# A fused windowed attention and softplus feed-forward kernel: the opening in another order, with clamps, low parts and divisions on GpSimd and chunk 1 laid out as chunk 0

## Chip, cores and metric

One core of one Trainium2 chip. The metric is the device time of one execution in microseconds (us), lower is better. The engines are PE (TensorE, matrix products), DVE (VectorE), ACT (ScalarE), POOL (GpSimd) and SP, which here only issues transfers. On each engine instructions run in the order in which the program has them; semaphores make them wait for other engines and for transfers.

## Reference

Attention over 8 batches, 8 heads, 576 positions and head dimension 64, in which heads 0 to 3 see a window of 32 positions and heads 4 to 7 every fourth position of a window of 128; its output (4608 tokens of 512 features) goes through a feed-forward layer of 2048 hidden features with softplus. All in float32.

```python
scores = scale * np.matmul(q, k.transpose(0, 1, 3, 2))
mask_plain = (rel >= 0) & (rel < window)
mask_dil = (rel >= 0) & (rel < window * dilation) & (rel % dilation == 0)
scores = np.where(masks[None, :, :, :], scores, -1000000000.0)
attn = np.exp(scores - np.max(scores, axis=-1, keepdims=True))
attn = attn / (np.sum(attn, axis=-1, keepdims=True) + 1e-09)
x = np.matmul(attn, v)                      # to 4608 x 512
h = x @ w_in
g = np.maximum(h, 0.0) + np.log1p(np.exp(-np.abs(h)))
out = g @ w_out
```

## The kernel before

The 4608 tokens are nine chunks of 512. A chunk has four attention groups of two heads (0 and 1 plain, 2 and 3 dilated); group n of the program is group n % 4 of chunk n // 4. A feed-forward slot is one chunk with one of 16 blocks of 128 hidden features (`ff`): in the first 22 slots these are blocks 0 to 4 of chunk 0, blocks 0 to 9 of chunk 1 and blocks 5 to 11 of chunk 0. [...]

The weights come as float64 words. Each of the 32 tiles (block `ff`, `i` = 0 for w_in, 1 for w_out) is decoded in seven steps by `decode_step` (L221): step 0 takes the absolute value on ACT (L229), step 1 clamps it to the exponents of float32 (L231), step 2 shifts (L235), steps 3 and 4 bring in the low bits and the sign (L240, L245), all on DVE; step 5 rounds to the high part on ACT (L252), step 6 subtracts it for the low part on DVE (L255).

The order of everything up to the 22nd slot is written out by hand, as a string of tokens, `OPENING` (L97), which the loop at L891 reads. Each token emits its instructions, and instructions that share an engine keep the order of the tokens. What follows is ordered by a planner, which starts at the 22nd slot and does not look back. The tokens, with n the group, i the slot and m or kt a quarter of a product:

- `q`, `k`, `v`, `m`, `r`: loads of queries, keys, values, masks and of one raw weight tile, issued by SP (only `k0` by ACT). `load_dma` (L195) lets six of the first 90 SP loads be under way: the seventh waits for the first.
- `S` scores with the mask added as a matmul (PE), `M` their maxima (DVE, L478), `N` or `Np` the factor 1/8 on DVE or POOL (L499), `E` eight exponentials with row sums (ACT, L518), `Ep` the sums' 1e-9 on POOL (L529), `Z` the reciprocal (DVE).
- `Pv` divides the 128 by 512 weights on DVE (L540); `T` turns them with four PE transposes, `C` copies them out of PSUM (ACT, L589); `V` is the product with the values (PE, L598), `Xt` a DVE transpose, `Xh` and `Xl` the high part (ACT, L714) and low part (DVE, L718) of the result. Quarters kt = 0 and 1 of a slot need groups 0 and 1 of its chunk, quarters 2 and 3 groups 2 and 3.
- `W` (`shares`, L651): in the geometry of the later chunks ("by head") the division comes after `V`, as eight ACT instructions that read the result from PSUM, each scaled by one column of reciprocals (L658); `Xt` then reads what they wrote. Before the change chunk 1 (groups 4 to 7) has this geometry, set by `BY_HEAD = 1`; chunk 0 divides with `Pv`.
- `H` is a quarter of the first product of a slot (three matmuls of 512 columns into `h_ps`), `A` three ACT passes for the softplus, `G` its last step (DVE, L773), `Gs` and `Gl` its high and low part (ACT L779, DVE L785), `O` a quarter of the second product (`o_ps`).
- `D0_ff_i` to `D5_ff_i` and `Dl` are the decode steps, `F` and `f` products that nobody reads.

POOL does only the small `Np` and `Ep` in the opening; later it subtracts weight blocks (L920). `PLACES` (L46) says in which PSUM banks a group has its scores, its turned weights and its result: `h` the two banks of `h_ps`, `o` those of `o_ps`, `a` the attention's own.

```python
            if self.by_head:
                by_block = self.v.rearrange("p i r d -> p (i r) d")
...
                divided = nc.scalar.activation(
                    out=self.x[:, n], in_=self.values_in[h][:, at_col : at_col + D], func=AF.Copy,
                    scale=self.ri[:, n : n + 1],
                )
```

Of the kernel before, what the change touches and what calls it, by code (L numbers as in the profile page):

```python
# [98 lines left out]
D3_1_0 q3 k3 S3 M3 E0 Pv1 q2 Np3 E3 Ep3 k2 S2 Z0 Pv0 T0 C0 q4 q5 m1 v0 k4 r2 r3 V0 D4_0_0 D5_0_0 M2 Np2 E2
Ep2 D4_1_0 D5_1_0 Z3 Pv3 Xt0 Xh0 D0_0_1 Dl0_0 S4 M4 Dl1_0 D0_2_0 T1 C1 Z2 Pv2 D1_0_1 D2_0_1 Np4 E4 Ep4  # L100
D1_2_0 Xl0 v1 V1 Xt1 Xh1 k5 D2_2_0 D3_2_0 S5 M5 Np5 Xl1 r4 v3 v2 r5 r6 q6 T2 D0_1_1 D3_0_1 D1_1_1 T3 C3 C2
H0_0 D2_1_1 E5 Ep5 F1_0 D4_2_0 D5_2_0 V3 Xt3 Xh3 V2 Xt2 Xl3 D4_0_1 D0_3_0 Xh2 Xl2 D1_3_0 Z4 D0_2_1 D1_2_1 Z5
T5 C5 H1_0 H0_1 T4 C4 D2_3_0 Dl2_0 D3_3_0 D4_3_0 D5_0_1 Dl0_1 H0_2 H0_3 A0 D3_1_1 G0 H1_1 H1_2 H1_3 A1 G1
D2_2_1 D5_3_0 Dl3_0 r7 k6 v4 v5 r8 q7 r9 r10 r11 S6 M6 Np6 V4 W4 D0_4_0 Gs0 Gs1 Xt4 Xh4 D4_1_1 Xl4 Gl0
D1_4_0 Gl1 D2_4_0 D3_2_1 D3_4_0 D4_4_0 D0_4_1 D5_1_1 Dl1_1 E6 Ep6 V5 W5 Xt5 H2_0 H2_1 H2_2 H3_0 H2_3 O0_0
D1_4_1 O0_1 H3_1 H3_2 H3_3 k7 S7 r12 r13 r14 O1_0 O1_1 O0_2 O0_3 M7 Np7 A2 G2 D4_2_1 O1_2 O1_3 D5_4_0 Dl4_0
A3 G3 Xh5 D2_4_1 Xl5 H4_0 H4_1 H4_2 H4_3 D3_4_1 D5_2_1 D0_3_1 Gs2 Gl2 D1_3_1 Dl2_1 O2_0 D2_3_1 D3_3_1 r15 E7
D4_4_1 Z6 D0_5_0 T6 H5_0 H5_1 D1_5_0 D0_6_1 v6 C6 V6 Ep7 Z7 O2_1 D1_6_1 D2_6_1 D4_3_1 A4 W6 Gs3 O2_2 O2_3 k8
v7 r16 r17 G4 D3_6_1 D4_6_1 Gl3 Xt6 T7 D0_5_1 D5_4_1 D1_5_1 D2_5_1 H6_0 H6_1 C7 V7 D5_3_1 Dl3_1 O3_0 O3_1
O3_2 O3_3 Xh6 Xl6 Gs4 W7 Gl4 Dl4_1 O4_0 O4_1 Xt7 Xh7 D2_5_0 D5_6_1 D0_7_0 D0_6_0 Xl7 H5_2 D3_5_0 D1_7_0  # L110
D3_5_1 D1_6_0 D4_5_1 D2_7_0 H5_3 A5 H6_2 H6_3 A6 m2 r18 q8 D4_5_0 D2_6_0 O4_2 r19 r20 K2 S8 G5 O4_3 G6
D3_7_0 D4_7_0 D3_6_0 Dl6_1 H7_0 H7_1 H8_0 H8_1 H7_2 H8_2 H7_3 H8_3 Gs5 K3 Gl5 K0 O5_0 D5_7_0 D5_5_1 Dl5_1
# [1980 lines left out]
```

## Time and profile before

| what | value |
|---|---|
| median of 3 runs | 823.47 us (821.29 to 823.65) |
| the profiled execution's own time | 822.52 us |
| its span, first to last instruction | 820.7 us |
| PE busy | 800.1 us, 97% |
| DVE busy | 648.1 us, 79% |
| ACT busy | 614.8 us, 75% |
| POOL busy | 63.9 us, 8% |
| moved by transfers | 198.45 MB, mean 242 GB/s |

All times inside the profile count from the span's start; 1.8 us of the execution's time lie outside it. "Busy" is a share of time, not of speed: a PE that runs at half clock counts as busy. The opening ends at about 166 us, when POOL begins to subtract weight blocks.

### The profile page before, as it was taken

What the parts mean: (1) busy time and instruction counts of PE and PEld (TensorE: products, weight loads), DVE (VectorE), ACT (ScalarE), POOL (GpSimd) and SP (SyncE); (2) the same over time, 40 slices, a digit from 0 to 9 for tenths busy, and PEclk for the clock granted to TensorE, in tenths of its full rate; (3) what the DMA queues carried; (4) which work ended last, traced back from release to release, by engine and by line L of the source; (5) the groups of instructions that cost most, each with busy time, mean ns of one, the idle gap of its engine ahead of it and who ended that gap; (6) DMA issues with size and microseconds to landing.
All of it is one profiled execution on the core that took longest, in us unless ns stands there. A gap on an engine that the chain in (4) does not pass through costs nothing.

```text
span 820.7 us, 19960 instructions
## 1 busy us (share of the span) xinstructions
PE 800.1 (97%) x7849; PEld 650.6 (79%) x7849; DVE 648.1 (79%) x945; ACT 614.8 (75%) x1468; POOL 63.9 (8%) x88
## 2 busy tenths in 40 slices
PE   5899999999999999999999999999999999999998
PEld 3677888888888877778888888888888888888886
DVE  5888988857587789778789998777798967667964
ACT  6999889867777777699899837887897345776732
POOL 1000000031335433000000000000000000000000
PEclk8799999999999999999999999999999999999999
DMA  8994835375999989657787968998776576666652
GB/s 299 314 313 138 283 101 177 121 241 186 339 297 342 318 317 341 234 173 224 255 274 246 310 226 272 288 308 289 242 244 210 189 242 205 204 193 212 223 198 85
DMA packets 105807, 198.45 MB, mean 242 GB/s; under 512 B 9585, under 2 KB 52593, under 8 KB 105713
## 3 DMA queue, kind: packets, MB, share of 16 engines
q1 hardware_dynamic: 105568, 196.88, 73.2%
q8 instruction: 62, 1.02, 0.5%
q14 instruction: 33, 0.26, 0.1%
q10 hardware_dynamic: 144, 0.29, 0.1%
HBM read 148.90 MB, written 48.23 MB: 240 GB/s over the span
## 4 chain that ended last, share of the span: by engine, by line
PE 94%; ACT 2%; DVE 2%; DMA 0%; issue 0%; POOL 0%; SPq 0%; DVEq 0%; ACTq 0%; POOLq 0%
PE o_ps L261 44%; PE h_ps L261 16%; PE h_y L261 14%; PE h_x L261 14%; PE sv_ps L261 5%; ACT s L518 1%; PE s_ps L261 1%; PE a_ps L261 1%; DMA k<-kpl 0%; PE t_ps L551 0%; DVE a L381 0%; ACT pt L658 0%; DVE s L381 0%; ACT pt L589 0%; DVE nm L478 0%
## 5 line engine op out<-in xcount | busy, mean ns | idle before, releaser
L261 PE MATMUL o_ps<-g,t 128*128 128x512 f32 x867 | 208.9, 389 | 0.0
L261 PEld LDWEIGHTS o_ps<-g,t 128*128 128x128 f32 x867 | 161.9, 188 | 34.3 <-DVE g L1502 0.2
L261 PE MATMUL o_ps<-g,parts 128*128 128x512 f32 x576 | 144.1, 393 | 0.2 <-DVE g L785 0.2
L261 PE MATMUL h_ps<-xh,parts 128*128 128x512 f32 x384 | 130.9, 397 | 1.1 <-DVE e L773 1.1
L261 PEld LDWEIGHTS o_ps<-g,parts 128*128 128x128 f32 x576 | 106.9, 188 | 24.0 <-DVE g L785 0.7
L1498 ACT CAST g<-stored 128x1024 fp32r<-128x1024 f32 x72 | 75.7, 1052 | 60.2 <-PE o_ps L261 56.6
L1502 DVE TENSOR_TENSOR g<-stored,g 128x1024 fp32r<-128x1024 f32 x72 | 87.8, 1221 | 26.1 <-ACT g L1498 25.9
L261 PEld LDWEIGHTS h_ps<-xh,parts 128*128 128x128 f32 x384 | 73.0, 190 | 17.4 <-DVE e L773 1.6
L518 ACT ACTIVATE s<-s,nm 128x64 f32<-128x64 f32 x224 | 75.7, 358 | 2.2 <-DVE nm L507 1.3
L261 PE MATMUL h_ps<-xl,parts 128*128 128x512 f32 x192 | 75.7, 394 | 0.0
L261 PE MATMUL h_y<-s,t 128*128 128x512 f32 x276 | 70.6, 391 | 0.0
L261 PE MATMUL h_x<-s,t 128*128 128x512 f32 x276 | 70.5, 391 | 0.0
L920 POOL TENSOR_TENSOR a<-a 128x256 f32<-128x256 f32 x64 | 56.8, 895 | 100.5 <-DVE a L915 81.5
L261 PEld LDWEIGHTS h_x<-s,t 128*128 128x128 f32 x276 | 51.6, 188 | 11.0
L261 PEld LDWEIGHTS h_y<-s,t 128*128 128x128 f32 x276 | 51.5, 188 | 10.9
L1478 DVE SCALAR_TENSOR_TENSOR stored<-stored,e 128x1024 f32<-128x1024 f32 x48 | 58.3, 1217 | 2.4 <-ACT e L1474 2.4
L1493 DVE TENSOR_TENSOR stored<-stored 128x1024 f32<-128x1024 f32 x48 | 58.1, 1215 | 0.2
L658 ACT ACTIVATE pt<-sv_ps,ri 128x64 f32<-128x64 f32 x224 | 49.0, 331 | 9.6 <-DVE s L484 6.7
L1468 ACT ACTIVATE e<-stored 128x1024 f32<-128x1024 f32 x48 | 50.6, 1056 | 3.0 <-DVE stored L1457 2.3
L1474 ACT ACTIVATE e<-e 128x1024 f32<-128x1024 f32 x48 | 50.7, 1061 | 1.0
L1471 ACT ACTIVATE e<-e 128x1024 f32<-128x1024 f32 x48 | 50.8, 1058 | 0.7
L773 DVE SCALAR_TENSOR_TENSOR e<-h_ps,e 128x512 f32<-128x512 f32 x48 | 32.9, 686 | 23.0 <-ACT e L1173 17.3
(112 smaller groups left out, 1260.0 us busy)
## 6 DMA issues: line engine op xcount, KB each, us to landing
t<-w_o SPq DMA_DIRECT2D x84, 512.0 KB, 4.3
raw<-w SPq DMA_DIRECT2D x64, 256.0 KB, 5.3
v<-vp SPq DMA_DIRECT2D x28, 512.0 KB, 5.5
t<-w SPq DMA_DIRECT2D x20, 512.0 KB, 4.1
t<-w_two SPq DMA_DIRECT2D x20, 512.0 KB, 4.4
k<-kl SPq DMA_DIRECT2D x31, 320.0 KB, 4.8
q<-qp SPq DMA_DIRECT2D x35, 256.0 KB, 4.2
w_o<-stage SPq DMA_DIRECT2D x32, 256.0 KB, 4.6
```

Source lines behind the costliest of these rows:

```text
L261: return tc.keep_in_program_order(nc.tensor.matmul(**kw))
L518: pin(nc.scalar.activation(out=self.blocks[:, t], in_=src, func=AF.Exp, bias=self.nm[:, t : t + 1], scale=1.0 / 8.0 if self.masked else 1. ...
L658: divided = nc.scalar.activation(out=self.x[:, n], in_=self.values_in[h][:, at_col : at_col + D], func=AF.Copy, scale=self.ri[:, n : n + 1],)
L773: pin(nc.vector.scalar_tensor_tensor(out=e, in0=tiles.pop(i), scalar=0.0, in1=e, op0=ALU.max, op1=ALU.add))
L920: pin(nc.gpsimd.tensor_tensor(out=out, in0=in0, in1=in1, op=ALU.subtract))
L1468: pin(nc.scalar.activation(out=es[key], in_=raw_g(*key), func=AF.Abs))
L1471: pin(nc.scalar.activation(out=es[key], in_=es[key], func=AF.Exp, scale=-1.0))
L1474: pin(nc.scalar.activation(out=es[key], in_=es[key], func=AF.Ln, bias=1.0))
L1478: pin(nc.vector.scalar_tensor_tensor(out=h, in0=h, scalar=0.0, in1=es.pop(key), op0=ALU.max, op1=ALU.add))
L1493: pin(nc.vector.tensor_tensor(out=raw_g(c, *PLACE[name]), in0=raw_g(c, *PLACE[a]), in1=raw_g(c, *PLACE[b]), op=op))
L1498: pin(nc.scalar.copy(out=set_of(k)[0], in_=raw_g(c, *PLACE[name])))
L1502: pin(nc.vector.tensor_tensor(out=low, in0=raw_g(c, *PLACE[name]), in1=high.bitcast(F32), op=ALU.subtract))
```

## The change

The string `OPENING` is another one, and so is `PLACES`. New tokens `Ba` and `Bl` are the clamp (step 1) and the low part (step 6) of a weight tile on POOL, the old token `P` divides on POOL. Counted in the new order, 19 clamps, 23 low parts and 5 divisions (groups 1, 2, 3, 4 and 7) are on POOL; groups 0, 5 and 6 divide on DVE. `BY_HEAD` is gone: chunk 1 is masked, divided, turned and read from PSUM as chunk 0 is, so its 32 ACT divisions go, and its `Xt` reads PSUM. The layout of its keys, queries and values on the host changes with it, the small tile `spread` is no longer loaded with the identity (128 by 640 instead of 128 by 768 elements of bfloat16), and its mask is added by a matmul with the identity over 128 rows instead of 32. The same loads, products and decode steps are done; one full product that nobody reads and the 21 small ones stand now at the program's start. The instructions behind the opening are the same ones in the same order on every engine.

```diff
-PLACES = "hoa oaa oao aoa haa ooa oaa aaa".split()
+PLACES = "aoa oao aoa hoo oaa hoa aaa oaa".split()
 FIRST = 2
-BY_HEAD = 1
...
 OPENING = """
-q1 k1 m0 S1 M1 q0 k0 S0 M0 N0 r0 r1 D0_0_0 D1_0_0 D2_0_0 D3_0_0 f21 Np1 E1 Ep1 Z1 D0_1_0 D1_1_0 D2_1_0
...
+q0 F1_1 m0 f21 k0 S0 M0 N0 k1 E0 k3 q3 S3 M3 Np3 E3 Ep3 m1 q1 q2 k2 S1 Z0 Pv0 T0 r0 r1 M1 Np1 k4 q4 Z3 P3 r2
...
-    def decode_step(ff, i, step):
+    def decode_step(ff, i, step, engine=None):
...
         elif step == 1:
-            pin(nc.vector.tensor_scalar(
+            pin((engine or nc.vector).tensor_scalar(
                 out=a, in0=a, scalar1=W_MIN, scalar2=W_MAX, op0=ALU.max, op1=ALU.min
...
             parts = words[key][3]
-            pin(nc.vector.tensor_tensor(
+            pin((engine or nc.vector).tensor_tensor(
                 out=parts[:, 1], in0=a, in1=parts[:, 0].bitcast(F32), op=ALU.subtract
...
-            self.own, self.masked, self.by_head = c == 0, c < 2, c >= BY_HEAD
+            self.own, self.masked = c == 0, c < 2
...
             first = True
-            if self.by_head:
+            if self.c >= FIRST:
                 by_block = self.v.rearrange("p i r d -> p (i r) d")
...
         "O": o_part,
+        "Ba": lambda ff, i: decode_step(ff, i, 1, nc.gpsimd),
+        "Bl": lambda ff, i: decode_step(ff, i, 6, nc.gpsimd),
         "Dl": lambda ff, i: decode_step(ff, i, 6),
```

What moves, at three places. First PE, from the last transposes ahead of the feed-forward products on (`t_ps` the transposes, `a_ps` the value products, `h_ps` the `H` quarters, `unread` a product that nobody reads). Before:

```order
L551 MATMUL t_ps<-ident,s 128x128 x8
L261 MATMUL h_ps<-xh,parts 128x512
L261 MATMUL h_ps<-xl,parts 128x512
L261 MATMUL h_ps<-xh,parts 128x512
L261 LDWEIGHTS consts
L261 MATMUL unread<-consts 128x512
L261 MATMUL a_ps<-v,pt 32x2x32 x64
L551 MATMUL t_ps<-ident,s 128x128 x4
```

and in the change:

```order
L542 MATMUL t_ps<-ident,s 128x128 x4
L259 MATMUL s_ps<-k,q 32x64 x32
L259 LDWEIGHTS consts
L259 MATMUL s_ps<-mask,consts 128x256
L542 MATMUL t_ps<-ident,s 128x128 x12
L259 MATMUL a_ps<-v,pt 32x2x32 x96
L259 MATMUL h_ps<-xh,parts 128x512
L259 MATMUL h_ps<-xl,parts 128x512
L259 MATMUL h_ps<-xh,parts 128x512 x2
```

The first `H` quarter no longer stands ahead of `V3` and `V2` but behind all three of `V1`, `V3`, `V2` (32 rows each), and the full unread product between them is gone from here.

Second POOL, from its first small instructions on. Before it has these alone:

```order
L499 TENSOR_SCALAR nm<-nm 128x8
L529 TENSOR_SCALAR sm<-sm 128x8
L499 TENSOR_SCALAR nm<-nm 128x8
L529 TENSOR_SCALAR sm<-sm 128x8 x5
L920 TENSOR_TENSOR a<-a 128x256 x64
```

and in the change, from its first division on:

```order
L531 TENSOR_TENSOR s<-s,ri 128x512
L490 TENSOR_SCALAR nm<-nm 128x8
L520 TENSOR_SCALAR sm<-sm 128x8
L229 TENSOR_SCALAR a<-a 128x512
L490 TENSOR_SCALAR nm<-nm 128x8
L531 TENSOR_TENSOR s<-s,ri 128x512 x2
L229 TENSOR_SCALAR a<-a 128x512
L531 TENSOR_TENSOR s<-s,ri 128x512
L253 TENSOR_TENSOR parts<-a,parts 128x512
```

The divisions (L531) stand in one queue with clamps (L229), low parts (L253) and the small factors (L490, L520) that ACT and DVE wait for.

Third ACT, from the first softplus (`e`) of the feed-forward on. Before:

```order
L766 ACTIVATE e<-h_ps 128x512
L767 ACTIVATE e<-e 128x512
L768 ACTIVATE e<-e 128x512
L252 CAST parts<-a 128x512
L658 ACTIVATE pt<-a_ps,ri 128x64 x8
L229 ACTIVATE a<-raw 128x512
L779 CAST g<-e 128x512 x2
L714 CAST xh<-s 128x8x64
```

and in the change:

```order
L753 ACTIVATE e<-h_ps 128x512
L754 ACTIVATE e<-e 128x512
L755 ACTIVATE e<-e 128x512
L580 COPY pt<-t_ps 128x512
L250 CAST parts<-a 128x512
L701 CAST xh<-s 128x8x64
L766 CAST g<-e 128x512
```

The eight divisions that read the result of `V` (L658) are gone; the copy of the turned weights (L580) takes a place of its own.

## Rows read from the trace of the kernel before

**Rows 1.** The page: span, busy time, and 40 slices of PE and its clock
```profile
span 820.7 us, 19960 instructions
PE 800.1 (97%) x7849; PEld 650.6 (79%) x7849; DVE 648.1 (79%) x945; ACT 614.8 (75%) x1468; POOL 63.9 (8%) x88
...
PE   5899999999999999999999999999999999999998
...
PEclk8799999999999999999999999999999999999999
```

**Rows 2.** Windows: stretch, length; busy PE, PEld, DVE, ACT, POOL; clock, DMA share, GB/s
```profile
14.00:27.70 13.70, 11.18 (x342) 8.28 (x342) 12.54 (x30) 12.46 (x61) 2.46 (x7) 0.50 0.93 305
27.70:39.60 11.90, 11.11 (x229) 8.03 (x228) 10.03 (x22) 10.61 (x31) 0.53 (x2) 0.91 0.88 297
39.60:48.85 9.25, 6.95 (x145) 5.48 (x144) 7.87 (x17) 9.22 (x37) 0.44 (x2) 0.82 0.98 324
48.85:166.00 117.15, 117.15 (x1115) 94.12 (x1114) 103.43 (x195) 102.49 (x267) 2.28 (x6) 1.00 0.56 179
166.00:300.00 134.00, 134.00 (x1497) 109.93 (x1496) 96.09 (x160) 100.09 (x290) 48.44 (x56) 1.00 0.87 290
```

**Rows 3.** PE's timeline to 50 us: start, length, engine, line, what [idle before <-releaser]
```profile
5.22 1.17 PE L261 MATMUL s_ps<-k,q 64*32 64x64 f32 x64 [5.22 <-DMA k<-kpl]
...
27.77 0.78 PE L261 MATMUL h_ps<-xh,parts 128*128 128x512 f32 x1
...
31.67 0.82 PE L261 MATMUL a_ps<-v,pt 64*32 64x64 f32 x60 [0.62 <-ACT s L518]
...
38.51 0.86 PE L261 MATMUL s_ps<-keys 64*32 64x64 f32 x64
...
39.61 0.86 PE L261 MATMUL a_ps<-v,pt 64*32 64x64 f32 x64
42.75 1.35 PE L261 MATMUL a_ps<-v,pt 64*32 64x64 f32 x64 [2.28 <-ACT pt L658]
44.03 0.79 PE L261 MATMUL h_ps<-xh,parts 128*128 128x512 f32 x1
...
48.85 1.52 PE L261 MATMUL o_ps<-g,parts 128*128 128x512 f32 x6
50.21 0.39 PE L261 MATMUL h_ps<-xh,parts 128*128 128x512 f32 x1
```

**Rows 4.** ACT's timeline, the first exponentials of a group to the next work; one W
```profile
9.11 0.30 ACT L518 ACTIVATE s<-s_ps,nm 128x64 f32<-128x64 f32 x1
...
11.43 0.72 ACT L229 ACTIVATE a<-raw 128x512 f32<-128x512 f32 x1
...
40.96 1.74 ACT L658 ACTIVATE pt<-a_ps,ri 128x64 f32<-128x64 f32 x8
```

**Rows 5.** Groups by line to 300 us: form, count | busy us, mean ns | idle before
```profile
L920 POOL TENSOR_TENSOR a<-a 128x256 f32<-128x256 f32 x56 | 48.7, 875 | 93.8 <-DVE a L915 75.1 <-DVE parts L942 13.2 <-DVE sm L529 3.2
L255 DVE TENSOR_TENSOR parts<-a,parts 128x512 fp32r<-128x512 f32 x32 | 21.5, 683 | 0.4 <-ACT parts L252 0.3
L915 DVE TENSOR_TENSOR a<-parts 128x512 f32<-128x512 f32 x28 | 20.6, 759 | 0.0
L231 DVE TENSOR_SCALAR a<-a 128x512 f32<-128x512 f32 x32 | 13.2, 412 | 1.1 <-ACT a L229 1.0
L942 DVE TENSOR_TENSOR stage<-a,stage 128x512 fp32r<-128x512 f32 x16 | 11.6, 748 | 0.0
L303 POOL MEMSET consts<- 128x512 bf16 x1 | 0.5, 525 | 0.3 <-POOLq L2075 0.3
```

**Rows 6.** POOL and DVE timelines: POOL with DVE quiet, POOL and DVE at once
```profile
199.06 0.75 POOL L920 TENSOR_TENSOR a<-a 128x256 f32<-128x256 f32 x1 [22.62 <-DVE a L915]
306.60 8.48 POOL L920 TENSOR_TENSOR a<-a 128x256 f32<-128x256 f32 x8 [6.38 <-DVE a L915]
310.25 1.23 DVE L785 TENSOR_TENSOR g<-e,g 128x512 fp32r<-128x512 f32 x1
```

More of the change, by code (lines that the diff above doesn't have):

```diff
@@ L97 @@
 OPENING = """
-q1 k1 m0 S1 M1 q0 k0 S0 M0 N0 r0 r1 D0_0_0 D1_0_0 D2_0_0 D3_0_0 f21 Np1 E1 Ep1 Z1 D0_1_0 D1_1_0 D2_1_0
[L99 to L112, printed above, removed]
@@ new lines @@
+r3 S2 M2 Np2 D0_0_0 D1_0_0 D2_0_0 E1 Ep1 D3_0_0 D0_1_0 Ba1_0 Z1 E2 Ep2 D4_0_0 D2_1_0 D0_0_1 Ba0_1 C0 D0_2_0 S4
+M4 D3_1_0 Np4 E4 Z2 P2 P1 Ba2_0 D2_0_1 D3_0_1 D4_0_1 v0 V0 Xt0 T3 C3 D4_1_0 Xh0 Ep4 Z4 Xl0 P4 q5 k5 S5 D5_0_0
+M5 Bl0_0 Np5 D2_2_0 T1 C1 D5_1_0 T2 C2 T4 C4 v1 r4 V1 D0_1_1 Xt1 D3_2_0 Bl1_0 Ba1_1 Xh1 Xl1 E5 Ep5 v3 V3 Xt3
+Xh3 v2 V2 Xt2 Xh2 D2_1_1 H1_0 H0_0 H0_1 q7 r5 r6 k7 H1_1 Xl3 Xl2 H1_2 H1_3 D4_2_0 H0_2 S7 D0_3_0 Z5 Pv5 D3_1_1
+D0_2_1 Ba3_0 D2_3_0 D3_3_0 D4_3_0 D5_0_1 Bl0_1 D5_2_0 Bl2_0 T5 A1 G1 D4_1_1 C5 H0_3 q6 v5 V5 Xt5 Ba2_1 A0 G0
@@ new lines @@
+M7 D5_3_0 Xh5 Xl5 H2_0 H2_1 k6 v4 V4 H2_2 Xt4 Bl3_0 H3_0 H3_1 Gs0 Gl0 D5_1_1 Dl1_1 Np7 E7 Ep7 Z7 r7 k8 r8 S6
+M6 Np6 H3_2 O0_0 O0_1 O0_2 H2_3 H3_3 Gs1 Xh4 Gl1 Xl4 O1_0 O1_1 O1_2 D0_4_0 Ba4_0 D2_2_1 D3_2_1 P7 D4_2_1
+D2_4_0 D0_3_1 E6 Ep6 Z6 v6 Pv6 T6 r9 r10 r11 r12 r13 A2 D0_4_1 D3_4_0 D1_3_1 D4_4_0 Ba4_1 O0_3 O1_3 D2_3_1 G2
+C6 V6 D5_4_0 D3_3_1 Xt6 Bl4_0 D0_5_0 Ba5_0 Gs2 Gl2 D5_2_1 Bl2_1 H4_0 H4_1 H4_2 A3 D2_5_0 D4_3_1 T7 Xh6 C7 H4_3
+D2_4_1 O2_0 G3 D3_4_1 Xl6 v7 q8 S8 m2 M8 r14 q9 r15 r16 r17 r18 m3 k9 O2_1 H5_0 A4 D0_7_0 Gs3 Gl3 D5_3_1 Bl3_1
@@ L301, in tile_windowed_attention_softplus_ffn @@
     masks, xt = {}, {}
-    still = low_and_g[:, P + SW :][:, : CH // 2].bitcast(BF16)
+    still = low_and_g[:, P // 2 + SW :][:, : CH // 2].bitcast(BF16)
     nc.gpsimd.memset(still, 0.0)
@@ L312, in load_mask @@
             nc.gpsimd.tensor_copy(out=ident, in_=identb)
-            masks[0] = consts[:, 2 * P :]
+            masks[0] = consts[:, P:]
             return
         masks[c] = wk.tile([P, 2 * SW], BF16, name="mask", bufs=1)
-        load_dma(out=masks[c], in_=cst[c, :, 2 * P :])
+        load_dma(out=masks[c], in_=cst[c, :, P:])
     def x_tiles(c):
@@ L453, in score @@
                 for r in range(2):
-                    if self.by_head:
-                        quad = slice(self.pr * SQ, (self.pr + 1) * SQ)
-                        matmul(
-                            out=self.banks[r][:, :SW], lhsT=spread[quad],
-                            rhs=masks[self.c][quad, r * SW : (r + 1) * SW], start=False, stop=True,
-                        )
-                        continue
                     matmul(
@@ L601, in weighted @@
             first = True
-            if self.by_head:
+            if self.c >= FIRST:
                 by_block = self.v.rearrange("p i r d -> p (i r) d")
@@ L662, in shares @@
                 pin(divided)
-                if n == 0 and self.c >= FIRST and partner(self.n) < len(groups):
+                if n == 0 and partner(self.n) < len(groups):
                     behind_of(divided, groups[partner(self.n)].scaled_by, "one engine at a time reads a bank")
         def unturned(self):
-            if self.by_head:
+            if self.c >= FIRST:
                 by_square = self.x.rearrange("p b (d k) -> p b d k", d=2)
-                x, j = x_half(self.c, self.dil) if self.c >= FIRST else None, self.j
-                if x is None:
-                    x, j = self.s.rearrange("p (d n) -> p d n", d=2), 0
-                    self.x = x
+                x = x_half(self.c, self.dil)
                 if self.dil:
                     pin(nc.vector.transpose(
-                        out=x[:, :, j * HALF : (j + 1) * HALF].rearrange("p d (b q) -> p b d q", q=SQ),
+                        out=x[:, :, self.j * HALF : (self.j + 1) * HALF].rearrange("p d (b q) -> p b d q", q=SQ),
                         in_=by_square,
@@ L681, in unturned @@
                     pin(nc.vector.transpose(
-                        out=by_block[:, j * NB : (j + 1) * NB],
+                        out=by_block[:, self.j * NB : (self.j + 1) * NB],
                         in_=by_square[:, :, d].rearrange("p b (c q) -> p b c q", c=DIL),
@@ L2023, in _layout @@
     ], axis=1)
-    qp[BY_HEAD:] = ql[BY_HEAD:].reshape(qp[BY_HEAD:].shape)
-    kl = np.empty((NCH - BY_HEAD, 2, 2, 2, D, 4, per + WIN), np.float32)
-    late = np.empty((NCH - BY_HEAD, 2, 2, 2, WKEYS, 2, 2, 4, D), np.float32)
-    for c in range(BY_HEAD, NCH):
+    qp[FIRST:] = ql[FIRST:].reshape(qp[FIRST:].shape)
+    kl = np.empty((NCH - FIRST, 2, 2, 2, D, 4, per + WIN), np.float32)
+    late = np.empty((NCH - FIRST, 2, 2, 2, WKEYS, 2, 2, 4, D), np.float32)
+    for c in range(FIRST, NCH):
         for j in range(2):
```

89 lines of the change are left out of this document (43 added, 46 removed).

## The prediction

> **What bounds the kernel now.** First the page [rows 1]: PE is busy in 97% of the span, and its slices and its clock are below full only at the start. So the question is how much of the start is lost, and whether the rest stays full. The windows [rows 2] split the opening. From 14 to 27.7 us PE's granted clock is 0.50, the lower of its two levels (1.2 of 2.4 GHz); it has only small attention products, with gaps, and ACT is busy 12.46 of 13.70 us. From 27.7 to 39.6 us the clock is 0.91 in the mean, from 39.6 to 48.85 us it is 0.82 and PE works 6.95 of 9.25 us. From 48.85 to 166 us PE is busy for all of the 117.15 us at full clock: nothing can be won there, only lost. What comes behind the opening is the same program. So the sum is over two steps, up to 39.6 and from there to 48.85 us, and a check that the third stretch stays full.
>
> PE's timeline [rows 3] shows the marks. The first scores wait for a load until 5.22 us, and the first `H` quarter runs at 27.77. At 39.61 us PE has done eight `H` quarters (slots 0 and 1), seven scores, six groups' transposes and four value products; call this mark A. Then it does `V4`, waits 2.28 us until ACT's divisions (L658) have emptied the bank, does `V5`, and from 44.03 us five `H` quarters until the first `O` at 48.85: mark B.
>
> **Step 1, to mark A.** The new order has done exactly the same work (with group 7's scores for group 6's) when `H0_3` is done, so the two times can be compared. PE must first pass `V1`, `V3` and `V2`, and `H0_0` also needs the banks that ACT's sixth block of exponentials (`E5`) reads.
>
> ACT's queue up to the end of `E5` has six `E`, five decode steps 0 and nine copies and casts. An `E` takes 2.32 us (from 9.11 to 11.43 [rows 4]). From the same part of ACT's timeline I take 0.57 and 0.52 us for the others, which overlap a little: 13.9 + 2.9 + 4.7 = 21.5 us. `E0` can begin 2.5 us behind the first scores, at 7.7; that gives 29.2 without a wait. I follow the waits through the order: 0.7 us before `E3` (keys and queries of group 3), 1.8 before the copies `C1`, `C2`, `C4`, whose transposes wait for three divisions in line on POOL (`P2`, `P1`, `P4`), and 0.8 for `Xt1`. `E5` ends at 32.5, and `H` begins about 32.1. Its 24 matmuls take 0.227 us each (six `O` matmuls from 48.85 to 50.21 [rows 3]), 5.5 us; the scores of group 7 take 1.1 (38.51 to 39.61 [rows 3]) and `T5` about 0.4: mark A at 39.1. If the clock is at the lower level for as long as before (0.91 of 11.9 us is 2.1 us at half speed, half of it lost), it is 40.2; with half of that, 39.7. Against 39.6 this step is worth nothing by itself.
>
> What is open is the price of POOL's 128 by 512 subtraction and division, which no row shows. The nearest row is its subtraction of 128 by 256: 0.75 us with DVE quiet, and 8.48 us for eight, 1.06 each, with DVE busy [rows 6]. Bounds are 0.75 (no dearer than half the size) and 2.1 (two, with DVE busy); the waits above were traced with 1.5, two of the quiet ones. I take 1.8, between 1.5 and 2.1, since DVE is near full here (12.54 of 13.70 us [rows 2]). Three in line: 3 x 0.3 = **+0.9 us**. The ends are 3 x 0.6 = +1.8 and, as `V2`'s values arrive at about 30 us whatever POOL does, -0.8 and no more. A clamp lies between 0.53 (a memset of as many columns [rows 5]) and 1.5; I take 0.75, and in these waits it stands beside other work. The Trainium skill (GPSIMD Engine Reference, Elementwise — side-by-side cycle accounting) gives 4497 ns for a two-input elementwise instruction of 2048 columns; a quarter, 1.12 us, is an estimate, and by it this step would be -0.8 and the sum 1.7 us lower. No row here has that size.
>
> **Step 2, from A to B.** Before, 9.25 us: `V4` 0.86, the rest of its wait for the bank, `V5` 1.35, and 15 matmuls from 44.03 to 48.85, 4.82 us [rows 3]. The wait comes from the geometry: the eight divisions of `W4` (1.74 us, from 40.96 [rows 4]) read the bank that `V5` writes, and they queued behind a softplus and a cast. In the new geometry DVE's transposes empty the bank, `V5` comes first, two `H` quarters stand between `V5` and `V4`, and the pause behind which the clock fell to 0.82 is gone. The same work at full clock: 2 x 0.86 + 15 x 0.227 = 5.1 us. That is **-4.1 us**. Other end: 0, if another wait takes its place. I checked the nearest: `H3_0` needs slot 0's softplus out of its bank; ACT's two softplus chains and `C5` end about 4.5 us after slot 1's last quarter, 42.8 with the last step on DVE, and PE gets there at about 44. So I take the full -4.1.
>
> **Step 3, 48.85 to 166 us.** DVE was busy 103.43 of 117.15 us, ACT 102.49 [rows 2]. The change takes 19 x 0.41 + 23 x 0.68 [rows 5] and one division off DVE, 24 us over the opening, and 4 x 1.74 = 7 us of divisions off ACT. It gives POOL 28 x 1.5 + 19 x 0.75 = 56 us. What POOL costs DVE is seen from 166 to 300 us, where POOL is busy 48.44 us [rows 2]: DVE's subtractions and sums there take 759 and 748 ns in the mean where the same size takes 683 [rows 5], 28 x 0.076 + 16 x 0.065 = 3.2 us. For 56 us and a denser DVE, 4 to 5 us. DVE is left with 19 us less work, ACT with 7 less. Nothing new for PE to wait for: **0**; the bad end is the second rival.
>
> The moved loads are the same bytes through one queue, the same ones before `V2`; the transfers' share is 0.93 in the first stretch [rows 2] in both orders, so nothing is won there. The mask's wider identity product and the two orders of unread products lie in PE's idle time at the start: 0, and without that cover under 1 us.
>
> **The sum.** +0.9 - 4.1 + 0 = -3.2 us. The profiled execution took 822.52 us, its span 820.7 and 1.8 around it; it is 0.95 below the median of the runs. It would take 819.3. Against the median of 823.47: **820.3 us**, 0.4% less. A measurement of this kernel tells about 0.3% (2.5 us) from no change, so the line is at 821.0.
>
> **Rivals.** *The gain is given back on POOL.* `E5` needs a factor (`Np5`) that stands on POOL behind `P4` and a low part, so POOL's queue sits in the one chain that leads to `H`. At 2.1 us each, three divisions and that low part are 4 x 0.6 = 2.4 us later than with 1.5, and if `H3_0` or `V4` waits another 1.5, the sum is -0.2: 823.3 us. For it speaks that POOL's eight in a row ran at 1.06 [rows 6]; against it that the mean of 56 was 0.875 [rows 5].
>
> *DVE is held up by POOL (slower).* When both wanted SBUF at 310.25 us, a DVE subtraction took 1.23 instead of 0.68 us [rows 5, 6]: 0.55 lost to a POOL instruction of 256 columns. If each POOL instruction cost that much, 28 x 1.1 + 19 x 0.55 = 41 us, DVE would have 41 - 24 = 17 us more work, against 13.7 us idle from 48.85 to 166: PE waits the other 3.3, so 826.8. It decides from a mean loss of (24 + 13.7) / 47 = 0.8 us per POOL instruction. Against it: the 0.07 us means above. The Trainium skill (SBUF — State Buffer, Who interferes with whom) says that a DVE instruction with two SBUF inputs and a GpSimd one that reads SBUF exclude each other, the later blocking until the first is done; the 1.23 us agree that it happens, the 759 ns that it is seldom the whole length.
>
> *The start shrinks as well.* If POOL's divisions take about 1 us and `H` meets a full clock, A comes at 38.3 (-1.3), B 4.1 earlier still, and ACT's freed 7 us take 1 or 2 us of small waits: 816.6.
>
> **Chances.** Forecast 0.44, gain given back 0.22, DVE held up 0.18, the start shrinks too 0.14; 0.02 for none of them. About three quarters of the first lie below 821.0: faster 0.34 + 0.14 = 0.48; no change 0.10 + 0.20 = 0.30; slower 0.18 and what is left, 0.22. The range takes in the third case and most of the second rival: 815.5 to 826.0. The likeliest case alone spans 818.5 to 822.5.
>
> **What would show it.** In the new profile: `V5` and `V4` wait for no ACT division, and the first `O` with slot 3's second quarter done before it stands near 45.6 us rather than 48.85; POOL's 512-column instructions near 1.5 to 1.8 us; DVE's subtractions near 0.7 in the mean; 48.85 to 166 us full. Wrong it is if `H` begins after 34 us, if a wait for POOL stands before `T4` or `E5` for over 2 us, or if PE's third stretch shows gaps.

## The result, and the profile after

The changed kernel takes **834.0 us** (median of 4 runs, 833.53 to 834.83) where the kernel before takes 822.9 in the same series: 1.0138 times as long, 95% interval 1.0120 to 1.0157. That is 11.4 us slower. The forecast was 820.3 us, within 815.5 to 826.0, with a chance of 0.22 for slower: wrong in sign and outside the range.

The page of the new kernel, beside [rows 1]:

```profile
span 832.0 us, 19955 instructions
...
PE 803.9 (97%) x7849; PEld 651.0 (78%) x7849; DVE 646.8 (78%) x903; ACT 609.0 (73%) x1436; POOL 143.2 (17%) x135
...
PE   5798989999999999999999999999999999999998
...
PEclk9799999999999999999999999999999999999999
```

PE's busy time has hardly moved (800.1 to 803.9 us); the span has grown by 11.3. The busy shares say nothing of where. The windows, cut at the same places as [rows 2] (busy PE, PEld, DVE, ACT, POOL; clock; transfers' share, GB/s), do:

```profile
14.00:27.70 13.70, 8.89 (x258) 5.78 (x242) 9.98 (x19) 11.31 (x56) 11.33 (x12) 0.98 0.98 338
27.70:39.60 11.90, 9.26 (x211) 7.29 (x212) 9.01 (x20) 8.53 (x27) 8.49 (x8) 0.60 0.90 299
39.60:48.85 9.25, 8.62 (x222) 6.45 (x221) 9.18 (x15) 7.28 (x16) 6.52 (x5) 1.00 0.38 115
48.85:166.00 117.15, 109.47 (x1072) 86.67 (x1071) 99.07 (x160) 94.10 (x246) 51.25 (x34) 0.99 0.58 185
166.00:300.00 134.00, 134.00 (x1437) 110.10 (x1436) 94.81 (x154) 98.53 (x271) 50.36 (x54) 1.00 0.83 276
```

The stretch from 48.85 to 166 us, in which PE had been busy for all of 117.15 us, now has 7.7 us without PE, and POOL is busy for 51 us of it. From 166 us on PE is full again.

Windows at fixed times compare different work. So I also took from each trace when PE has as much work behind it as the kernel before had at a mark. Work is summed at full-clock prices: 0.227 us for a product of 512 columns, 0.120 for 256, 0.057 for a transpose, 0.0122 for a small product. Each row is one trace, and whether starts or ends are counted moves a figure by up to 0.5 us. The lag behind the kernel before, in us:

| kernel | A, 39.6 | B, 48.85 | 60 | 70 | 80 | 100 | 120 | 166 |
|---|---|---|---|---|---|---|---|---|
| forecast | +0.9 | -3.2 | | | | | | -3.2 |
| the change | +3.9 | +0.9 | +2.7 | +3.6 | +5.5 | +7.4 | +11.3 | +10.8 |
| e1, all on DVE | +4.1 | +1.4 | +3.1 | +2.6 | +3.2 | +3.4 | +2.7 | +2.5 |
| e12 | +3.1 | -0.3 | +0.3 | +0.1 | +0.3 | +0.4 | -0.3 | -0.5 |

The first step is 3.0 us worse than forecast, the second wins 3.0 of the 4.1 forecast, and the third, priced at nothing, costs 9.9. PE's timeline (start, length, what, idle before and who ended it) shows the places:

```profile
35.21 0.80 PE L259 MATMUL h_ps<-xh,parts 128*128 128x512 f32 x1
...
43.47 0.86 PE L259 MATMUL a_ps<-v,pt 64*32 64x64 f32 x64
44.95 0.50 PE L259 MATMUL h_ps<-xh,parts 128*128 128x512 f32 x1 [0.63 <-DVE e L760]
...
46.55 0.86 PE L259 MATMUL a_ps<-v,pt 64*32 64x64 f32 x64
...
79.41 0.73 PE L259 MATMUL o_ps<-g,parts 128*128 128x512 f32 x2 [1.82 <-POOL parts L253]
...
96.75 1.20 PE L259 MATMUL o_ps<-g,parts 128*128 128x512 f32 x4 [1.27 <-DVE g L772]
...
122.01 0.50 PE L259 MATMUL h_ps<-xh,parts 128*128 128x512 f32 x1 [2.61 <-DVE e L760]
```

`V5` (43.47) and `V4` (46.55) wait for nobody, as forecast; the 2.28 us wait of [rows 3] is gone. But `H` begins at 35.2 us, and later a low part on GpSimd and two DVE instructions come late. Behind the last of these waits PE's clock is at its lower level for a while (0.83 in the mean; 1.00 in the windows before and behind):

```profile
120.00:130.00 10.00, 7.99 (x28) 6.46 (x29) 9.04 (x15) 7.04 (x12) 6.86 (x4) 0.83 0.08 27
```

PE's waits behind 48.85 us add up to 7.6 us, and a clock of 0.83 over 10 us costs another 1.7: together 9.3 of the 9.9 us.

What POOL's instructions cost, and what DVE's cost beside them, is in the groups by form up to 170 us (busy us, mean ns | idle before):

```profile
L229 POOL TENSOR_SCALAR a<-a 128x512 f32<-128x512 f32 x19 | 40.7, 2146 | 12.6 <-ACT a L227 8.8 <-DMA keys<-kdl 1.7 <-DMA turned<-squares 1.6
L253 POOL TENSOR_TENSOR parts<-a,parts 128x512 fp32r<-128x512 f32 x19 | 28.2, 1487 | 38.8 <-ACT parts L250 38.8
L531 POOL TENSOR_TENSOR s<-s,ri 128x512 f32<-128x512 f32 x5 | 6.3, 1261 | 0.4 <-DVE ri L528 0.3
...
L238 DVE SCALAR_TENSOR_TENSOR a<-raw,a 128x512 int32<-128x512 int32 x32 | 28.6, 898 | 0.4
L243 DVE SCALAR_TENSOR_TENSOR a<-raw,a 128x512 int32<-128x512 int32 x31 | 24.0, 776 | 0.2
L233 DVE TENSOR_SCALAR a<-a 128x512 int32<-128x512 int32 x32 | 21.0, 661 | 11.2 <-POOL a L229 10.9
...
L760 DVE SCALAR_TENSOR_TENSOR e<-h_ps,e 128x512 f32<-128x512 f32 x20 | 13.6, 681 | 4.8 <-ACT e L755 4.8
```

Three things stand there. The clamp costs GpSimd 2.15 us, where DVE needs 0.41 [rows 5] and the forecast had 0.75. DVE's steps 2 to 4 have grown from 0.42, 0.69 and 0.69 us to 0.66, 0.90 and 0.78. And DVE stood 10.9 us waiting for clamps, which the forecast did not have at all. The softplus step (L760), which reads PSUM, is as long as ever.

The largest wait, at 119 us, shows all of it at work. POOL first, then DVE:

```profile
114.93 3.03 POOL L253 TENSOR_TENSOR parts<-a,parts 128x512 fp32r<-128x512 f32 x1 [6.74 <-ACT parts L250]
117.93 1.91 POOL L229 TENSOR_SCALAR a<-a 128x512 f32<-128x512 f32 x1
119.81 1.26 POOL L253 TENSOR_TENSOR parts<-a,parts 128x512 fp32r<-128x512 f32 x1
...
114.92 0.69 DVE L238 SCALAR_TENSOR_TENSOR a<-raw,a 128x512 int32<-128x512 int32 x1
115.52 0.69 DVE L772 TENSOR_TENSOR g<-e,g 128x512 fp32r<-128x512 f32 x1
116.12 0.68 DVE L243 SCALAR_TENSOR_TENSOR a<-raw,a 128x512 int32<-128x512 int32 x1
119.88 1.48 DVE L233 TENSOR_SCALAR a<-a 128x512 int32<-128x512 int32 x1 [3.07 <-POOL a L229]
121.28 0.68 DVE L760 SCALAR_TENSOR_TENSOR e<-h_ps,e 128x512 f32<-128x512 f32 x1
```

A low part on POOL takes 3.03 us instead of 1.26, because three DVE instructions in a row run beside it: they end at 116.8, and 1.16 us of the 3.03 come behind them. The clamp stands behind it in POOL's queue. DVE's shift waits for the clamp, and `e`, which PE needs, waits behind the shift on DVE although its own data had been there since 116.7 us, when ACT's last pass (L755) ended. When the shift may start, POOL starts the next low part at the same moment, and the shift takes 1.48 us instead of 0.42.

### The profile page after: what moved, and what is told of

It is laid out like the page before. It is cut to its first block, busy times and chain, and to the rows that moved or that the text cites. A ratio compares the mean times of both kernels' runs of the same rounds, so it can differ in the third digit from the quotient of the medians.

```text
span 832.0 us, 19955 instructions
## 1 busy us (share of the span) xinstructions
PE 803.9 (97%) x7849; PEld 651.0 (78%) x7849; DVE 646.8 (78%) x903; ACT 609.0 (73%) x1436; POOL 143.2 (17%) x135
## 4 chain that ended last, share of the span: by engine, by line
PE 83%; POOL 2%; DVE 2%; issue 2%; ACT 1%; DMA 1%; SPq 0%; DVEq 0%; POOLq 0%; ACTq 0%
PE o_ps L259 40%; PE h_y L259 14%; PE h_x L259 14%; PE h_ps L259 12%; PE sv_ps L259 5%; POOL a L229 1%; POOL parts L253 1%; DMA raw<-w 1%; ACT s L509 1%; DVE g L772 0%; DVE e L760 0%; DVE a L379 0%; DVE s L379 0%; DVE s L475 0%; ACT a L227 0%
## 5 line engine op out<-in xcount | busy, mean ns | idle before, releaser
L259 PE MATMUL o_ps<-g,parts 128*128 128x512 f32 x576 | 146.4, 394 | 3.7 <-POOL parts L253 2.1
L259 PE MATMUL h_ps<-xh,parts 128*128 128x512 f32 x384 | 133.3, 398 | 4.8 <-DVE e L760 4.4
L259 PEld LDWEIGHTS h_x<-s,t 128*128 128x128 f32 x276 | 51.6, 188 | 10.9
L760 DVE SCALAR_TENSOR_TENSOR e<-h_ps,e 128x512 f32<-128x512 f32 x48 | 32.8, 684 | 19.9 <-ACT e L1162 15.1
```

Of the source, the lines that this page charges most:

```text
L259: return tc.keep_in_program_order(nc.tensor.matmul(**kw))
L760: pin(nc.vector.scalar_tensor_tensor(out=e, in0=tiles.pop(i), scalar=0.0, in1=e, op0=ALU.max, op1=ALU.add))
```

## Experiments

All ratios are to the kernel before on the same chip; a difference in us is the difference of ratios times 822.9.

### What of the loss is GpSimd's: e1 to e4

Only tokens are exchanged, in place (`Ba` by `D1_`, `Bl` by `Dl`, `P` by `Pv`): e1 takes all three kinds back to DVE, e2 to e4 one each.

```diff
-r3 S2 M2 Np2 D0_0_0 D1_0_0 D2_0_0 E1 Ep1 D3_0_0 D0_1_0 Ba1_0 Z1 E2 Ep2 D4_0_0 D2_1_0 D0_0_1 Ba0_1 C0 D0_2_0 S4
+r3 S2 M2 Np2 D0_0_0 D1_0_0 D2_0_0 E1 Ep1 D3_0_0 D0_1_0 D1_1_0 Z1 E2 Ep2 D4_0_0 D2_1_0 D0_0_1 D1_0_1 C0 D0_2_0 S4
...
```

> The new order and geometry with all 19 clamps, 23 low parts and 5 divisions back on DVE, nothing else changed. Theory A (what stands on GpSimd is the whole loss): the order and geometry give the gain that was forecast, 819 to 822 us. Theory B (the order itself loses, whoever does the work): it stays at 830 to 835. A value of 823 to 829 says that both have a part. Under A, DVE's subtractions and shifts in the first 166 us are back at 0.42 and 0.69 us in the mean, and no wait of PE behind 50 us is over 1.5 us.

> The new kernel with its 19 clamps back on DVE; low parts and divisions stay on GpSimd. Theory C (the clamps are the cost: 2.15 us each on GpSimd against 0.41 on DVE, first in the chain of a weight tile, and each holding DVE up): two thirds of the 11 us come back, 824 to 827 us, and the waits at 79, 96 and 119 us go. Theory D (the low parts are: 1.49 us, last in the chain, directly ahead of PE): 831 to 833.

> The new kernel with its 23 low parts back on DVE; clamps and divisions stay on GpSimd. Theory C (clamps): 829 to 833 us, the wait of 2.6 us at 119 us shrinks because the low part ahead of that clamp is gone, but the waits of DVE for clamps (3.5 us at 87, 1.6 us at 94) stay. Theory D (low parts): 824 to 827.

> The new kernel with its 5 softmax divisions back on DVE; clamps and low parts stay on GpSimd. Theory E (the three divisions in line hold the start up, as my rival on GpSimd had it): the first H quarter begins 2 to 3 us sooner than at 35.2 us and the time is 831 to 832. Theory C: the start waits for clamps as well, the time is 833 to 835.

Measured: e1 1.0021 (1.0010 to 1.0033), e2 1.0030 (1.0018 to 1.0042), e3 1.0064 (1.0049 to 1.0079), e4 1.0138 (1.0123 to 1.0153).

So 9.6 of the 11.4 us are GpSimd's (1.0138 less 1.0021), and 1.7 are the order's own, which was to win 3. The five divisions cost nothing that can be measured: with them back on DVE `H` begins at 36.30 us, no sooner than the 35.21 of the change, and theory E falls. Taking the clamps back gives 8.9 us, taking the low parts back 6.1, and both together no more than 9.6. They are not two prices that add: with divisions on POOL in each, clamps alone there cost 3.5 us (e3 against e1), low parts alone 0.7 (e2 against e1), which is within the noise. The rest, 5.4 us, comes only when both are on POOL. The rows at 119 us show one way, the shared queue; in e3, without low parts there, that wait is gone, as its expectation said, and in e2 no wait of PE behind 50 us is over 0.9 us. How much of the 5.4 us the queue makes was not measured by itself. e1 lies where both parts have a share, e2 in theory C's range, e3 between C's and D's: C is right that the clamps weigh most, and neither theory had the coupling.

### Holding DVE up, or standing in the chain: e8, e9, e10

A clamp on POOL can hurt in two ways: its instruction blocks DVE's, or its result comes late. e8 takes e1 and adds 19 clamps that nobody needs, each released by the step 0 that released the real one. e10 adds 23 such subtractions as well, each released by the step 5 of its tile. Both kinds read the small identity tile and write a bfloat16 scratch tile, so they are stand-ins for the real ones, not copies.

```diff
+    def clamp_and_idle(ff, i):
+        decode_step(ff, i, 1)
+        ins = tc.keep_in_program_order(nc.gpsimd.tensor_scalar(
+            out=still.rearrange("p (n c) -> p n c", c=P), in0=ident.unsqueeze(1).to_broadcast([P, DM // P, P]), scalar1=W_MIN, scalar2=W_MAX, op0=ALU.max, op1=ALU.min
+        ))
...
-        "Ba": lambda ff, i: decode_step(ff, i, 1, nc.gpsimd),
+        "Ba": clamp_and_idle,
```

> The new order with everything on DVE, and beside it GpSimd does 19 more clamps of 128 by 512 that nobody needs, each released by the same step 0 as the real one and in the same place of its queue. Theory L (clamps on GpSimd cost by holding DVE up): DVE's steps 2 to 4 get longer as in the new kernel, and most of the 3.6 us come by which clamps on GpSimd alone were slower than everything on DVE: 827 to 828.5 us. Theory M (they cost by their own 2 us in the chain of a weight tile): 824.5 to 825.5.

> Everything on DVE, and beside it GpSimd does 19 clamps and 23 subtractions of 128 by 512 that nobody needs, each released by the same ACT step as the real one, in its place of the queue. Theory L (what GpSimd does costs by holding DVE up, whoever needs the result): of the 9.5 us between everything on DVE and the new kernel more than half come: 829.5 us or more. Theory M (it costs by standing in the chain of a weight tile, a low part behind a clamp in one queue): little more than with the idle clamps alone, 826 to 828.5 us.

Measured: e8 1.0048 (1.0031 to 1.0065), which is 2.2 us above e1 and just short of theory L's range, and e10 1.0202 (1.0188 to 1.0217), 14.9 us above e1. e8 by itself decides little: its interval touches e1's, and steps 2 to 4, which theory L had grow, hardly do (0.45, 0.70 and 0.71 us); DVE's clamp does (0.52). Groups by form of e10 up to 170 us (five of its 23 subtractions come later):

```profile
L224 POOL TENSOR_SCALAR consts<-ident 128x512 bf16<-128x512 f32 x19 | 40.4, 2128 | 16.5 <-ACT a L244 13.2 <-ACT ob L825 2.5
L228 POOL TENSOR_TENSOR consts<-ident 128x512 bf16<-128x512 f32 x18 | 23.4, 1300 | 37.5 <-ACT parts L268 36.8
...
L271 DVE TENSOR_TENSOR parts<-a,parts 128x512 fp32r<-128x512 f32 x27 | 22.4, 834 | 2.2 <-ACT parts L268 2.2
L247 DVE TENSOR_SCALAR a<-a 128x512 f32<-128x512 f32 x32 | 19.6, 618 | 0.5 <-ACT a L244 0.5
```

Nobody waits for these results, and yet DVE's low part goes from 0.683 to 0.834 us in the mean and its clamp from 0.41 to 0.62. The small factors `Np` and `Ep` that stand behind them in POOL's queue are no other way out: up to 170 us ACT and DVE wait 3.3 us for those, in e1 3.2. PE's waits from 48.85 to 170 us, all for DVE, go from 2.1 us in e1 to 9.9. Theory L holds: work on GpSimd that no engine uses slows the kernel by 14.9 us, more than the new kernel's GpSimd work does, which at least takes work off DVE.

e9 goes the other way. It leaves the kernel before as it was and moves the same 19 clamps to GpSimd.

```diff
-            pin(nc.vector.tensor_scalar(
+            pin((engine or nc.vector).tensor_scalar(
...
+        "Ba": lambda ff, i: decode_step(ff, i, 1, nc.gpsimd),
```

> The kernel before, in its own order and geometry, with the clamps of the same 19 weight tiles moved to GpSimd. If the price of the clamps is their own and not of the new order, they cost about what they cost in the new order alone, 3 to 5 us: 826 to 828 us. If the old order has the slack to hide them, 823 to 824.5; if its tighter chains take them worse, over 829.

Measured: 1.0119 (1.0103 to 1.0135), 9.8 us: its third case, the tighter chains take them worse. Its groups:

```profile
L235 DVE TENSOR_SCALAR a<-a 128x512 int32<-128x512 int32 x32 | 14.1, 444 | 17.8 <-POOL a L231 17.6
...
L231 POOL TENSOR_SCALAR a<-a 128x512 f32<-128x512 f32 x19 | 38.7, 2044 | 54.0 <-ACT a L229 53.6
```

The shift behind the clamp takes 0.444 us, nearly what it took before. But DVE stands still for 17.6 us ahead of it, with its later work queued behind. So here the loss is mostly the late result, theory M. By the measure of the table above, 6.3 of the 9.8 us are lost before mark A, where the chain goes through the attention: ACT's exponentials wait 6.7 us for `Np` on POOL, 0.6 in the kernel before. It does so three times; the longest is this (ACT's timeline):

```profile
34.35 0.32 ACT L518 ACTIVATE s<-s_ps,nm 128x64 f32<-128x64 f32 x1 [2.85 <-POOL nm L499]
```

Twice the cause is that the maxima `M` stand on DVE behind a shift that waits for a clamp, and once (1.78 us, at 26.98) `Np` itself stands behind a clamp in POOL's queue. Both ways, blocking and lateness, exist; that it depends on what DVE has next which one shows is my reading, not a test.

An account of DVE up to 166 us puts them together. *Freed* is what was moved away from it in the whole opening (0.41 us a clamp, 0.68 a low part, 0.69 a division), relative to e1, for e9 to the kernel before; four of the change's 23 low parts come behind 166 us. *Held up* sums, over DVE instructions more than 0.06 us above their form's median in the kernel before, what they took more. *Stood* is its idle time ahead of the shift that waits for POOL.

| kernel | freed | held up | stood | left over | time |
|---|---|---|---|---|---|
| the change | 27.0 | 18.5 | 10.9 | +2.4 | +9.6 |
| e2, low parts and divisions | 19.2 | 15.2 | 0 | -4.0 | +0.7 |
| e3, clamps and divisions | 11.3 | 6.5 | 7.2 | +2.4 | +3.5 |
| e8, idle clamps | 0 | 5.5 | 0 | +5.5 | +2.2 |
| e10, idle both | 0 | 18.6 | 0 | +18.6 | +14.9 |
| e9, clamps in the old order | 7.8 | 2.7 | 17.6 | +12.5 | +9.8 |

In the lower five rows the time lies within 5 us of what is left over, which is rough. In the change it is further off: DVE is only 2.4 us worse off, and the time is up by 9.6. What PE's rows show beside it: the low parts, now behind clamps in POOL's queue, come late for PE themselves (2.5 us in all, 1.82 of them at 79.4), and DVE is late at places that PE waits for (1.27 us at 95, 2.61 at 119, and the slower clock behind that).

### What GpSimd pays for: e7

```diff
-            pin((engine or nc.vector).tensor_scalar(
-                out=a, in0=a, scalar1=W_MIN, scalar2=W_MAX, op0=ALU.max, op1=ALU.min
-            ))
+            if engine is not None:
+                pin(engine.tensor_scalar(out=a, in0=a, scalar1=W_MIN, scalar2=None, op0=ALU.max))
...
```

> The new kernel, with its 19 clamps on GpSimd cut to one operation, the maximum with the lower bound; the upper bound is left out there. Theory N (GpSimd pays for each operation of an instruction): 1.92 us of a quiet clamp fall to 1.2 to 1.4, and the time to 829 to 832 us. Theory O (it pays for the elements alone): the clamp stays at 1.9 and the time at 834.

Measured: 1.0091 (1.0065 to 1.0116), 3.9 us less than the change. A clamp with DVE quiet (POOL's timeline):

```profile
115.83 1.48 POOL L230 TENSOR_SCALAR a<-a 128x512 f32<-128x512 f32 x1
```

One operation takes 1.48 us, two take 1.91 (117.93 above), against 1.26 for a subtraction of two inputs. Theory N is right in kind, not in size: the second operation costs 0.43 us. If the first costs as much, 1.05 us would be there without either, an estimate that no run tests. Over 19 clamps 0.43 us is 8.2 us of POOL's time, and about half of it reaches the end. By the account above it comes by way of lateness: DVE is held up no less than in the change (20.4 us), but stands 8.1 instead of 10.9 us for clamps.

### Why the start was late: e5, e6, e13

With everything on DVE the work of mark A is still 4.1 us late. PE's timeline of e1 shows odd stops:

```profile
11.51 0.45 PE L542 MATMUL t_ps<-ident,s 128*128 128x128 f32 x1
13.20 0.80 PE L542 MATMUL t_ps<-ident,s 128*128 128x128 f32 x3 [1.24 <-ACT s L509]
...
16.30 1.42 PE L259 MATMUL s_ps<-k,q 64*32 64x64 f32 x57 [0.66 <-DMA q<-qp]
18.45 0.43 PE L259 MATMUL s_ps<-k,q 64*32 64x64 f32 x7 [0.72 <-issue]
...
31.37 0.89 PE L259 MATMUL a_ps<-v,pt 64*32 64x64 f32 x34 [0.67 <-PE a_ps L259]
34.01 1.62 PE L259 MATMUL a_ps<-v,pt 64*32 64x64 f32 x94 [1.75 <-issue]
```

They split groups of transposes or small products that need the same data. Counting all of PE's instructions in the trace, those that only wait for a semaphore too, they stand behind the 449th, 705th, 961st and 1217th: 256 apart. The page of the changed kernel has this row of transfers (queue and kind: packets, MB, share):

```profile
q8 instruction: 62, 1.02, 0.5%
```

PE's 15,918 instructions in its trace (2 x 7849 matmuls and weight loads, 220 others, nearly all waits) make 257 for each of the 62 packets. The trace has each packet's time, too: in e1 a q8 packet of 16 KB lands at 11.9, 17.0, 24.6 and 33.0 us, each 1.1 to 1.4 us before one of the four stops ends. e5 is e1 without 20 of the small unread products, so that blocks end elsewhere in the work. e6 is e1 with four loads under way, e13 is e12, a later version (below), with five.

```diff
-q0 F1_1 m0 f21 k0 S0 M0 N0 k1 E0 ...
+q0 F1_1 m0 f1 k0 S0 M0 N0 k1 E0 ...
```

```diff
-DEPTH = 6
+DEPTH = 4
```

> The new order with everything on DVE, and 20 of its 21 small unread products at the start left out: 40 instructions fewer on PE ahead of everything else. With all on DVE, PE stood still ahead of its 449th, 705th, 961st and 1217th instruction in the profile, for 1.65, 1.04, 1.52 and 1.97 us, each in the midst of one product's small matmuls and each 256 instructions behind the one before. Theory F (PE's instructions arrive late, in blocks of 256): the stops keep their numbers, and so lie 40 instructions further on in the work. Theory G (they are waits for data of these products): they stay at the same places of the work, at numbers lower by 40. The time itself may go either way, 822 to 827 us.

> The new order with everything on DVE, and at most four of the first loads under way instead of six. Theory F (the blocks of PE's instructions queue behind the loads in the transfer engines): the four stops, 6.2 us together, shrink to 3 us or less, the first H quarter begins 1.5 to 2.5 us sooner than at 35.6 us, and the time is 821.5 to 823.5 us against 824.7. Theory G (waits for data): the loads land later and the time is 825 to 828.

> The kernel of e12 with at most five of the first loads under way. With six the work of mark A was done 3.1 us later than in the kernel before. If PE's late instruction blocks hold that step, their way past fewer queued loads is shorter, the stops shrink, and mark A comes sooner by 0.5 to 1.5 us: 821.3 to 822.5. If the loads hold it, their later landing shows: 823.5 to 825.

e5 measured 1.0022 (1.0005 to 1.0039), the time of e1. Its PE timeline:

```profile
12.55 0.53 PE L259 MATMUL s_ps<-k,q 64*32 64x64 f32 x17
13.42 0.71 PE L259 MATMUL s_ps<-k,q 64*32 64x64 f32 x47 [0.35 <-issue]
...
30.61 1.17 PE L259 MATMUL a_ps<-v,pt 64*32 64x64 f32 x54 [0.62 <-PE a_ps L259]
33.23 1.21 PE L259 MATMUL a_ps<-v,pt 64*32 64x64 f32 x74 [1.45 <-issue]
```

The first stop is still behind number 449, but inside the scores of group 2 instead of the transposes of group 0. The last is still behind number 1217, but after 54 of that value product's 64 pieces instead of 34: 20 pieces, 40 instructions further on. The other two are gone: shortly ahead of them PE now waits 2.43 and 1.16 us for other things. That is theory F as far as the late blocks go. In all the traces, every stop of PE over 0.25 us that the profile puts down to no data ("issue") lies at a multiple of 256 from these numbers or one instruction beside it, and ends 1.1 to 1.6 us after a q8 packet of 16 KB landed. The old order (the kernel before and e9), with six loads as well, has none.

But they are not what the start is made of. e6 measured 1.0051 (1.0032 to 1.0070). Its PE timeline:

```profile
24.35 1.52 PE L259 MATMUL a_ps<-v,pt 64*32 64x64 f32 x64 [4.36 <-DMA v<-vp]
...
32.37 2.15 PE L259 MATMUL a_ps<-v,pt 64*32 64x64 f32 x128 [0.62 <-PE a_ps L259]
```

The stops of the start are gone (128 pieces in one row; two others show at 52.5 and 72.1 us, 1.09 and 0.88 us long), the first `H` comes at 34.56 instead of 35.56 us, and still mark A is 4.3 us late, because the first value product waits 4.36 us for its load. The time got worse, as theory G had it. e13 measured 1.0008 (0.9994 to 1.0021), not to be told from e12's 1.0002. Its two stops are 1.42 and 1.75 us long, longer than e12's 0.43 and 0.60 with six loads, and its lag at mark A is 3.8, e12's 3.1. So the late blocks are shown, and that four loads under way cost more than the stops. That the loads hold the blocks up is not shown, since five loads did not shorten the stops, and how much of the 3 us the stops hold is open. e1 and e11, whose tokens are the same up to there, differ in the lag at A by 0.9 us (4.1 and 5.0).

### A better version: e11, e12

e11 is e1 with low parts drawn ahead on DVE:

```diff
-Xt4 Dl3_0
+Dl3_0 Xt4
...
-D5_4_0 D3_3_1 Xt6 Dl4_0
+D5_4_0 Dl4_0 D3_3_1 Xt6
...
-D4_5_0 D1_7_0 D0_6_1 D1_6_1 Gs4 Dl4_1 D2_7_0 Gl4
+D4_5_0 D0_6_1 Gs4 Dl4_1 Gl4 D1_7_0 D1_6_1 D2_7_0
```

e12 adds e5's edit and a weight step behind the mask sum of group 8 (`D3_4_1` behind `M8`).

> Everything on DVE, with three steps moved on DVE alone: the low parts of tiles 3_0 and 4_0 ahead of a transpose that waits for a value product, and the low part of 4_1 and the low part of slot 4's softplus ahead of two clamps and a shift. Theory H (with everything on DVE the new order still loses where a low part queues on DVE behind work that could wait: PE waits 0.7, 1.0 and 0.4 us there, and runs at the lower clock behind the first two): 821 to 823 us, below the kernel before or equal to it. Rival K (the time goes at the start, and what is won here is lost at the next wait): 824 to 825.5.

> The kernel with everything on DVE and three low parts sooner, with two more edits: 20 small unread products less at the start, so that PE's stops at its 705th and 961st instruction fall where it waits anyway, and a weight step on DVE behind the mask sum of group 8, for which the value product at 66.6 us waits 0.5 us. Theory F says that the stops at the start cost net what e5 won up to 40 us, 0.5 to 1 us; with the half us of the second edit 821.5 to 822.8, below the kernel before by 0 to 0.2%. If the start is bound by the loads and by ACT whatever the stops do: 823 to 824.

Measured: e11 1.0006 (0.9995 to 1.0017), 1.2 us better than e1 and level with the kernel before; e12 1.0002 (0.9990 to 1.0015), level too. e11 lies between its two theories, e12, at 823, at the edge of its second. No version beat the kernel before by what can be measured; e12 is 11 us faster than the change with the same geometry and nearly the same order.

## Why the prediction was wrong

**What bounds the kernel** held: the loss is PE's, lies ahead of 166 us, and what comes behind is the same.

**Step 1 (forecast +0.9, measured +3.9)** failed. `H` was to begin at 32.1 us, 33.0 with the +0.9, and began at 35.2. The copy chain and the sixth exponentials were too early in the working: `E5` runs from 32.85 us, where it was to end at 32.5. In the change ACT waits 1.66 us for `Np4`, which stands behind two clamps on POOL, a wait that the working did not have (ACT's timeline):

```profile
22.33 0.32 ACT L509 ACTIVATE s<-s_ps,nm 128x64 f32<-128x64 f32 x1 [1.66 <-POOL nm L490]
...
32.85 0.31 ACT L509 ACTIVATE s<-s_ps,nm 128x64 f32<-128x64 f32 x1
```

From `H` to mark A it took 8.3 us where the working had 7.0 and half a us for the clock, which was 0.60 from 27.7 to 39.6 us. But e1, without clamps on POOL, is as late: other waits take their place there, among them PE's late instruction blocks and the load for the first value product, whose net prices the runs did not settle. The price taken for POOL's three divisions, 1.8 us, was too high (1.26 in the mean of all five, 1.04 for the first, with DVE quiet), and taking the divisions off POOL wins nothing (e4), although `T4` does wait 1.57 us for one there. The estimate of 1.12 us for that size, from the Trainium skill (GPSIMD Engine Reference, Elementwise — side-by-side cycle accounting), was nearer than the 1.8 that I worked out from a row of half the size.

**Step 2 (forecast -4.1, measured -3.0)** held in mechanism: `V5` and `V4` wait for nobody and the clock is 1.00. Of the 1.1 us that are missing, 0.63 are a wait for a softplus step on DVE; the rest I have not traced.

**Step 3 (forecast 0, measured +9.9)** is the step that failed most; 1.1 of the 9.9 are the order's own (e1). "Nothing new for PE to wait for" was wrong: PE waits 7.6 us there, where the kernel before has no wait at all: 4.6 for DVE, 2.5 for low parts on POOL and 0.5 for ACT. Two terms under it were wrong. The clamp was put at 0.75 us between bounds of 0.53 and 1.5; it took 2.15 (1.91 at the least), outside the bounds, since a memset reads nothing and I had no row with one input and two operations. And "DVE is left with 19 us less work" came from one row's mean, 0.07 us lost beside POOL, taken from a stretch in which POOL had 56 small subtractions; here DVE was held up for 18.5 of the 27 us freed, and stood 10.9 us for clamps. I had followed POOL's queue into the chain only as far as `H`.

**The rival "DVE held up by POOL"** named the mechanism, but at 826.8, and I gave it 0.18. The 826.8 also left out the 3.2 us that the first two steps were to win; with them it would have been 823.6, so that even this rival had no case near 834. Its test was a sum: 0.8 us lost per instruction on POOL before DVE's 13.7 idle us were used up. Measured were (18.5 + 10.9) / 47 = 0.63, below the test, and the kernel is 11 us slower. Idle time elsewhere on DVE's line is no cover for a step that PE waits for at 95 and 119 us. The other rival on POOL, the gain given back there, needed 2.1 us for each division and low part; they took 1.26 and 1.49. The Trainium skill's rule that I set beside it (SBUF — State Buffer, Who interferes with whom) is what the trace shows here: whole instructions blocked, 26 DVE instructions by 0.7 us in the mean; the means of [rows 5] had hidden it. But only 15 of the 26 have two inputs in SBUF; 11 are ten shifts and a clamp, with one input, of which the rule as I had set it down says nothing.

**Of the three signs that I had named** for being wrong two showed: `H` after 34 us, and gaps in the third stretch. The third did not: the wait for POOL before `T4` is 1.57 us, not over 2.
